# Attention kernel: inputs laid out with channels on rows, key sums by matmul, GpSimd's order written out

## The chip, the cores and the metric

The kernel runs on one core of a Trainium2 chip as a single launch. The metric is the device time of one execution in microseconds (us), lower is better; runs are compared by their medians. The engines are named as in the profile: PE is TensorE (PEld its weight loads), DVE is VectorE, ACT is ScalarE, POOL is GpSimd, SP is the queue of SyncE, which issues nearly all DMAs.

## The reference

Three stages follow each other: linear attention with an exponential feature map, a dense MLP, and a mixture of eight experts of which each token uses one. The change touches the attention, and in the others only the order of tokens.

```python
# q, k, v: (4, 8, 576, 64), w_phi: (64, 128)
def phi(x):
    proj = einsum('bhsd,df->bhsf', x, w_phi)
    proj = proj - max(abs(proj), axis=-1, keepdims=True)
    return concatenate([exp(proj), exp(-proj)], axis=-1)
q_p, k_p = phi(q), phi(k)
kv  = einsum('bhsf,bhsd->bhfd', k_p, v)
z   = sum(k_p, axis=2)
num = einsum('bhsf,bhfd->bhsd', q_p, kv)
den = einsum('bhsf,bhf->bhs', q_p, z)[..., None] + 1e-06
x = (num / den)                       # -> (2304 tokens, 512)
# MLP: h = x @ w_in; x = (h * clip(h+3,0,6)/6) @ w_out
# experts: argmax gate picks 1 of 8; relu(x @ w1[e]) @ w2[e], scaled by the gates
```

## The kernel before

**Units.** The attention works on 16 units: one batch entry and one pair of heads each. A unit holds 2 x 576 rows of q and as many of k, as nine blocks of 128 rows and two heads (blocks 0 to 3 keys, 4 the last 64 positions of both, 5 to 8 queries). Products that need more than one pass of precision are made of two halves: a value is rounded to `hi` (type fp32r), and `lo` is what is left.

**One unit's steps**, by the two-letter names that the order string `seq` uses:

- T0 to T2 (`tr_in`): TensorE transposes three blocks each (L273), so that channels lie on the partitions; ACT copies the result out of PSUM as `hi` (L276), DVE subtracts for `lo` (L278).
- P0 to P4 (`proj`): three matmuls per block (hi by hi, hi by lo, lo by hi; L294 to L296); DVE takes the largest absolute value (L300) and subtracts it (L302), giving `dd`.
- E0 to E2 (`kexp`): ACT makes both exponentials of the keys, `kp` (L309 to L313).
- S (`z_sum`): POOL adds the four key blocks of a head into `ks` (L332 to L334).
- KV (`kv_mm`): ten matmuls of `kp` with `v` into `pkv` (L324). Z (`z_mm`): four matmuls with ones, on `ks` and on the last block, into the other half of `pkv` (L342), in four groups of 32 columns of the array. C copies `pkv` out (L349); KT transposes it (L356) and makes `kvz` (ACT, L360) and `zs` (DVE, L362).
- Q0 to Q2 (`q_tr`): the queries are transposed (L378, L383); ACT makes their exponentials `qp` (L381, L386).
- N0, N1 (`num`): numerators (L431), copied into `xT` (L439). D (`den`): denominators (L396), `dn` on DVE (L406), of which four rows go by DMA into the 128-row tile `rt` (L408).
- R (`den2`, for the unit before): reciprocal (L413), DMA to DRAM, two DMAs that spread it over the partitions as `rr` (L418), and a multiply of `xT` by it on POOL (L421).
- w (`split_w`): one of the 16 pieces of the MLP's first weight half, read as 64-bit floats, becomes two fp32r halves: four DVE operations (L157, L160, L162, L164) beside a square on ACT (L158); L164 zeroes what is too small. Then a copy (L172, for two pieces on ACT, L170) and a subtraction (L173) on POOL.

**Order.** Within `tc.manual_schedule` the instructions of the engines named run in the order in which the code emits them; here these are TensorE, DVE and ACT. POOL's order and that of the DMAs on SP are the framework's. Iteration `it` runs KV, Z, Q, N, D of unit `it`, P and E of unit `it+1`, T of unit `it+2`, and loads unit `it+3` with seven DMAs. Two iterations (-2, -1) fill the pipeline; the last two have strings of their own. PSUM banks are given out by tags: two for transposes, three for P, one for KV, two for N and D.

**Afterwards** the MLP starts with six chunks of 384 tokens: L540 is its first matmul. It needs the first weight half, and while it runs its first chunk the second half is converted by the same `split_w`. Then tokens are listed by expert, and the experts run. `pieces` gives the rows of DRAM for a block of columns, as the columns of a unit are not in the order of tokens.

## Time and profile before

| | before |
|---|---|
| median of three runs | 943.39 us (943.04, 943.39, 945.1) |
| profiled execution | 944.11 us, of it span 942.0 us |
| mean granted clock of TensorE | 0.992 |
| busy share: PE / PEld / DVE / ACT / POOL | 96% / 79% / 65% / 55% / 37% |
| moved by DMA | 85.72 MB, mean 91 GB/s |

Times in the rows are us from the span's start unless marked ns. The share of a whole span is a mean over stages with different limits: in the attention DVE is nearly as busy as TensorE, in the experts it is not, so a stage has to be read by itself.

### The profile page before, as it was taken

What the parts mean: (1) busy time and instruction counts of PE and PEld (TensorE: products, weight loads), DVE (VectorE), ACT (ScalarE), POOL (GpSimd) and SP (SyncE); (2) the same over time, 40 slices, a digit from 0 to 9 for tenths busy, and PEclk for the clock granted to TensorE, in tenths of its full rate; (3) what the DMA queues carried; (4) which work ended last, traced back from release to release, by engine and by line L of the source; (5) the groups of instructions that cost most, each with busy time, mean ns of one, the idle gap of its engine ahead of it and who ended that gap; (6) DMA issues with size and microseconds to landing.
All of it is one profiled execution on the core that took longest, in us unless ns stands there. A gap on an engine that the chain in (4) does not pass through costs nothing. (4 is left out here: it accounts for less than half of the span.)

```text
span 942.0 us, 14999 instructions
## 1 busy us (share of the span) xinstructions
PE 903.5 (96%) x5250; PEld 740.3 (79%) x5250; DVE 615.8 (65%) x1033; ACT 518.9 (55%) x919; POOL 350.4 (37%) x246
## 2 busy tenths in 40 slices
...
GB/s 162 183 140 134 138 124 138 97 49 132 117 133 5 1 68 1 1 34 1 1 35 0 1 34 1 28 185 21 58 54 215 175 252 42 215 107 204 194 142 19
DMA packets 54349, 85.72 MB, mean 91 GB/s; under 512 B 18037, under 2 KB 30969, under 8 KB 54269
## 3 DMA queue, kind: packets, MB, share of 16 engines
...
## 5 line engine op out<-in xcount | busy, mean ns | idle before, releaser
L543 DVE SCALAR_TENSOR_TENSOR t<-t,ph 128x384 f32<-128x384 f32 x96 | 53.0, 552 | 159.8 <-ACT t L542 159.8
L542 ACT ACTIVATE t<-ph,b 128x384 f32<-128x384 f32 x96 | 55.7, 580 | 164.9 <-PE ph L540 164.9
L680 POOL DMA_INDIRECT lst<-ids,pi x18 | 17.8, 986 | 237.2 <-DVE pi L677 230.8
L548 ACT ACTIVATE gh<-t 128x384 fp32r<-128x384 f32 x96 | 50.4, 525 | 84.4 <-DVE t L543 81.6
L847 DVE TENSOR_TENSOR wl<-raw,wh 128x1024 fp32r<-128x1024 f32 x63 | 76.1, 1245 | 9.5 <-ACT wh L846 9.3
L552 DVE TENSOR_TENSOR gl<-t,gh 128x384 fp32r<-128x384 f32 x86 | 48.0, 558 | 46.2 <-ACT gh L548 45.6
L846 ACT ACTIVATE wh<-raw 128x1024 fp32r<-128x1024 f32 x72 | 73.0, 1070 | 4.8 <-DMA raw<-in_moe_w 4.8
L540 PE MATMUL ph<-xh,wi0A 128*128 128x384 f32 x192 | 67.6, 352 | 1.6 <-DVE t L543 1.6
L540 PE MATMUL ph<-xl,wi0A 128*128 128x384 f32 x192 | 64.7, 337 | 1.2 <-DVE xl L531 1.2
L540 PE MATMUL ph<-xh,wi1B 128*128 128x384 f32 x192 | 64.6, 336 | 0.9 <-POOL wi1B L173 0.9
L540 PE MATMUL ph<-xh,wi0B 128*128 128x384 f32 x192 | 64.8, 338 | 0.1
L540 PE MATMUL ph<-xh,wi1A 128*128 128x384 f32 x192 | 64.6, 337 | 0.0
L540 PE MATMUL ph<-xl,wi0B 128*128 128x384 f32 x192 | 64.4, 335 | 0.0
L567 PE MATMUL po<-wo1B,gh 128*128 128x512 f32 x144 | 57.3, 398 | 1.3 <-POOL wo1B L173 1.3
L300 DVE TENSOR_REDUCE mx<-pj 128x4 f32<-128x512 f32 (+1 forms) x80 | 50.4, 630 | 11.9 <-PE pj L296 11.8
L567 PE MATMUL po<-wo0B,gh 128*128 128x512 f32 x144 | 57.0, 396 | 0.6 <-ACT wo0B L170 0.6
L567 PE MATMUL po<-wo1A,gh 128*128 128x512 f32 x144 | 56.6, 393 | 0.0
L567 PE MATMUL po<-wo0A,gh 128*128 128x512 f32 x144 | 56.6, 393 | 0.0
L332 POOL TENSOR_TENSOR ks<-kp 128x512 f32<-128x512 f32 x16 | 20.9, 1307 | 89.0 <-ACT kp L310 89.0
L847 DVE TENSOR_TENSOR wi1A<-raw,wi0A 128x1024 fp32r<-128x1024 f32 x42 | 50.0, 1221 | 5.6 <-ACT wi0A L846 5.5
L847 DVE TENSOR_TENSOR wo1A<-raw,wo0A 128x1024 fp32r<-128x1024 f32 x41 | 50.6, 1265 | 3.6 <-ACT wo0A L846 3.5
L302 DVE TENSOR_TENSOR dd<-pj,mx 128x512 f32<-128x512 f32 (+1 forms) x80 | 51.0, 638 | 2.8
...
## 6 DMA issues: line engine op xcount, KB each, us to landing
...
```

Source lines behind the costliest of these rows:

```text
L300: nc.vector.tensor_reduce(m, pv, axis=AX.X, op=ALU.max, apply_absolute_value=True)
L302: nc.vector.tensor_sub(dv, pv, m.unsqueeze(2).broadcast_to([P, 2 * n, P]))
L332: nc.gpsimd.tensor_add(ks, k4[:, :, 0, 0], k4[:, :, 0, 1])
L540: nc.tensor.matmul(ph[:, 0:T], l[:, d, fs], r[:, d, :], start=(d == 0 and i == 0), stop=(d == 3 and i == 2))
L542: nc.scalar.activation(g, ph[:, 0:T], AF.Relu, bias=b3)
L543: nc.vector.scalar_tensor_tensor(g, g, 6.0, ph[:, 0:T], op0=ALU.min, op1=ALU.mult)
L548: nc.scalar.activation(gh, g, AF.Copy)
L552: (nc.gpsimd if 4 < n < 15 else nc.vector).tensor_sub(gl, g, gh.bitcast(F32))
L567: nc.tensor.matmul(pos[c][j], l[:, js], wo[r], start=(f == 0 and r == 0 and l is gh), stop=(f == 15 and l is gl))
L680: sc = nc.gpsimd.indirect_dma_start(lst, bass.IndirectOffsetOnAxis(ap=pi[:, j : j + 1], axis=0), ids[:, m : m + 1], None, bounds_check=NL - 1,
L846: nc.scalar.activation(hi, raw[i], AF.Copy)
L847: (nc.gpsimd if i == 7 or (s, i) == (0, 6) else nc.vector).tensor_sub(lo, raw[i], hi.bitcast(F32))
```

## The change

- The host lays the inputs out anew (`lay_out`): q and k of a unit as one array `qk` of 128 rows (two heads by 64 channels) by nine blocks of 128 positions, v as ten blocks with the zeros of the last two already in place, `w_phi` as the block-diagonal matrix. A unit is two DMAs (unit 0's `qk` three). Columns are now in the order of tokens, so `pieces` goes.
- T goes. In its place H (`cut`): POOL copies three blocks of `qk` to `hi` and subtracts for `lo`. For unit 0 (`h`) ACT and DVE do it. One filling iteration remains.
- S goes. Z has ten matmuls instead of four: every key block is summed with ones on TensorE.
- `split_w` for the first weight half: ACT takes the absolute value, POOL the maximum with a bound (`TINY`), and three DVE operations remain; the copy is POOL's for all pieces. For the second half nothing changes.
- All PSUM tiles of the attention share one tag of eight banks.
- POOL joins the engines with a written order. The order strings are new: KV first, the five P in one block, H behind them, R in two parts (the reciprocal and its DMAs early, the multiply late). In `kv_tr`, DVE's `zs` comes before ACT's `kvz`.

```diff
--- before.py
+++ after.py
...
@@ -154,23 +138,35 @@
     yield
     f = pool.tile([P, n], U32, tag=tags[0], bufs=tags[2], name=f"f_{nm}")
     m = pool.tile([P, n], F32, tag=tags[1], bufs=tags[2], name=f"m_{nm}")
-    nc.vector.tensor_scalar(f, hw, 3, 0x3FFFFFFF, op0=ALU.logical_shift_left, op1=ALU.bitwise_and)
-    nc.scalar.activation(m, hw.bitcast(F32), AF.Square)
-    yield
-    nc.vector.scalar_tensor_tensor(f, lw, 29, f, op0=ALU.logical_shift_right, op1=ALU.bitwise_or)
-    yield
-    nc.vector.scalar_tensor_tensor(f, hw, 0xC0000000, f, op0=ALU.bitwise_and, op1=ALU.bitwise_or)
-    yield
-    nc.vector.scalar_tensor_tensor(
-        m, m, TINY * TINY, f.bitcast(F32), op0=ALU.is_ge, op1=ALU.mult
-    )
+    if act:
+        nc.vector.tensor_scalar(f, hw, 3, 0x3FFFFFFF, op0=ALU.logical_shift_left, op1=ALU.bitwise_and)
+        nc.scalar.activation(m, hw.bitcast(F32), AF.Square)
+        yield
+        nc.vector.scalar_tensor_tensor(f, lw, 29, f, op0=ALU.logical_shift_right, op1=ALU.bitwise_or)
+        yield
+        nc.vector.scalar_tensor_tensor(f, hw, 0xC0000000, f, op0=ALU.bitwise_and, op1=ALU.bitwise_or)
+        yield
+        nc.vector.scalar_tensor_tensor(
+            m, m, TINYB * TINYB, f.bitcast(F32), op0=ALU.is_ge, op1=ALU.mult
+        )
+        f = m
+    else:
+        nc.scalar.activation(m, hw.bitcast(F32), AF.Abs)
+        nc.gpsimd.tensor_scalar(m, m, TINY, None, op0=ALU.max)
+        yield
+        nc.vector.tensor_scalar(f, m.bitcast(U32), 3, 0x3FFFFFFF, op0=ALU.logical_shift_left, op1=ALU.bitwise_and)
+        yield
+        nc.vector.scalar_tensor_tensor(f, lw, 29, f, op0=ALU.logical_shift_right, op1=ALU.bitwise_or)
+        yield
+        nc.vector.scalar_tensor_tensor(f, hw, 0xC0000000, f, op0=ALU.bitwise_and, op1=ALU.bitwise_or)
+        f = f.bitcast(F32)
     if act == 1:
         yield
     if act:
-        nc.scalar.activation(hi, m, AF.Copy)
+        nc.scalar.activation(hi, f, AF.Copy)
     else:
-        nc.gpsimd.tensor_copy(hi, m)
-    nc.gpsimd.tensor_sub(lo, m, hi.bitcast(F32))
+        nc.gpsimd.tensor_copy(hi, f)
+    nc.gpsimd.tensor_sub(lo, f, hi.bitcast(F32))
 
 
 def weight_tiles(pool, nm):
...
@@ -210,72 +206,43 @@
         pl = E(name="apl", bufs=2, side="left")
         p3 = E(name="ap3", bufs=1, side="left")
         ps = E(name="aps", bufs=1, space=PS)
-        pn = E(name="apn", bufs=1, space=PS)
-        q, k, v, w = a["q"], a["k"], a["v"], a["w_phi"]
         wbd = cst.tile([P, 256], F32, name="wbd")
-        nc.vector.memset(wbd, 0.0)
         whi = cst.tile([P, 256], F32R, name="whi")
         wlo = cst.tile([P, 256], F32R, name="wlo")
         ones = cst.tile([P, 3, 32], F32, name="ones")
         nc.gpsimd.memset(ones, 1.0)
         nc.gpsimd.memset(ones[64:128, 1, :], 0.0)
         nc.gpsimd.memset(ones[0:64, 2, :], 0.0)
-        vms = []
-        for i in range(4):
-            vm = cst.tile([P, 2, 64], F32, name=f"vm{i}")
-            nc.gpsimd.memset(vm, 0.0)
-            vms.append(vm)
         rscr = tc.dram_tile([NU, P, 9], F32, name="rscr")
 
         def load(u):
-            b, hp = divmod(u, 4)
-            ts = {}
-            for nm, src in (("k", k), ("q", q), ("v", v)):
-                t = p2.tile([P, 2, 4, 64], F32, tag="l" + nm, bufs=4 if nm == "v" else 2, name=f"{nm}{u}")
-                nc.sync.dma_start(
-                    t.rearrange("p h r d -> p h (r d)"),
-                    src[b, 2 * hp : 2 * hp + 2, 0:512, :].rearrange("h (p r) d -> p h (r d)", r=4),
-                )
-                ts[nm] = t
-                if nm == "k" and u == 0:
-                    nc.sync.dma_start(wbd[0:64, 0:128], w)
-                    nc.sync.dma_start(wbd[64:128, 128:256], w)
-                if nm == "q":
-                    qkm = load_rest(u, b, hp)
-            for h in range(2):
-                nc.sync.dma_start(vms[u % 4][64 * h : 64 * h + 64, h, :], v[b, 2 * hp + h, 512:576, :])
-            return [ts["q"], ts["k"], ts["v"], qkm, vms[u % 4]]
-
-        def load_rest(u, b, hp):
-            qkm = p2.tile([P, 2, 64], F32, tag="qkm", name=f"qkm{u}")
-            for i, src in enumerate((q, k)):
-                nc.sync.dma_start(qkm[:, i, :], src[b, 2 * hp : 2 * hp + 2, 512:576, :])
-            return qkm
+            x = p2.tile([P, 9, P], F32, tag="qk", bufs=2, name=f"qk{u}")
+            if u == 0:
+                nc.sync.dma_start(wbd, a["w_phi"])
+                for g in range(3):
+                    nc.sync.dma_start(x[:, 3 * g : 3 * g + 3], a["qk"][u][:, 384 * g : 384 * g + 384])
+            else:
+                nc.sync.dma_start(x.rearrange("p n t -> p (n t)"), a["qk"][u])
+            t = p2.tile([P, 10, 64], F32, tag="lv", bufs=4, name=f"v{u}")
+            nc.sync.dma_start(t.rearrange("p n d -> p (n d)"), a["v"][u])
+            return [x, t]
 
         hl, st, bk, rts = {}, {}, {}, {}
 
-        def tr_in(u, g):
-            Q, K, V, QKM, vm = lds[u]
+        def cut(u, g):
+            x = lds[u][0]
             if g == 0:
                 hl[u] = (
                     p1.tile([P, 9, P], F32R, tag="hi", name=f"hi{u}"),
                     p1.tile([P, 9, P], F32R, tag="lo", name=f"lo{u}"),
                 )
             hi, lo = hl[u]
-            pt = ps.tile([P, 512], F32, tag="tr", bufs=2, name=f"pt{u}_{g}")
-            for j in range(3):
-                n = 3 * g + j
-                if n == 4:
-                    src = QKM
-                else:
-                    t, n = (K, n) if n < 4 else (Q, n - 5)
-                    src = t[:, n // 2, 2 * (n % 2) : 2 * (n % 2) + 2, :]
-                nc.tensor.transpose(pt[:, j * P : (j + 1) * P], src.rearrange("p a d -> p (a d)"), ident)
-            yield
             sl = slice(3 * g, 3 * g + 3)
-            nc.scalar.activation(hi[:, sl, :], pt[:, 0:384], AF.Copy)
-            yield
-            nc.vector.tensor_sub(lo[:, sl, :], pt[:, 0:384], hi[:, sl, :].bitcast(F32))
+            if u:
+                nc.gpsimd.tensor_copy(hi[:, sl], x[:, sl])
+            else:
+                nc.scalar.activation(hi[:, sl], x[:, sl], AF.Copy)
+            (nc.gpsimd if u else nc.vector).tensor_sub(lo[:, sl], x[:, sl], hi[:, sl].bitcast(F32))
 
         def proj(u, g):
             hi, lo = hl[u]
@@ -288,7 +255,7 @@
             dd, kp, mx = st[u]
             grp = [2 * g, 2 * g + 1] if g < 2 else ([4] if g == 2 else [2 * g - 1, 2 * g])
             n = len(grp)
-            pj = ps.tile([P, 512], F32, tag="pj", bufs=3, name=f"pj{u}_{g}")
+            pj = ps.tile([P, 512], F32, tag="b", bufs=8, name=f"pj{u}_{g}")
             for j, bl in enumerate(grp):
                 o = pj[:, 256 * j : 256 * j + 256]
                 nc.tensor.matmul(o, hi[:, bl, :], whi, start=True, stop=False)
@@ -313,35 +280,34 @@
                 nc.scalar.activation(kp[:, 4, 0, 1, :], dd[:, 4, 1, :], AF.Exp, scale=-1.0)
 
         def kv_mm(u):
-            V, vm = lds[u][2], lds[u][4]
+            V = lds[u][1]
             kp = st[u][1]
-            pkv = ps.tile([P, 512], F32, tag="kv", bufs=1, name=f"pkv{u}")
+            pkv = ps.tile([P, 512], F32, tag="b", bufs=8, name=f"pkv{u}")
             bk.setdefault(u, {})["pkv"] = pkv
             for r in range(5):
                 for h in range(2):
-                    l = V[:, h, r, :] if r < 4 else vm[:, h, :]
+                    l = V[:, 4 * h + r] if r < 4 else V[:, 8 + h]
                     m = kp[:, 2 * h + r // 2, r % 2] if r < 4 else kp[:, 4, 0]
                     nc.tensor.matmul(
                         pkv[64 * h : 64 * h + 64, 0:256], l, m.rearrange("p s f -> p (s f)"), start=(r == 0), stop=(r == 4)
                     )
 
-        def z_sum(u):
-            kp = st[u][1]
-            ks = p2.tile([P, 2, 2 * P], F32, tag="kvs", bufs=1, name=f"ks{u}")
-            k4 = kp[:, 0:4].rearrange("p (h a) e s f -> p h a e (s f)", h=2)
-            nc.gpsimd.tensor_add(ks, k4[:, :, 0, 0], k4[:, :, 0, 1])
-            nc.gpsimd.tensor_add(ks, ks, k4[:, :, 1, 0])
-            nc.gpsimd.tensor_add(ks, ks, k4[:, :, 1, 1])
-            bk.setdefault(u, {})["ks"] = ks
-
         def z_mm(u):
-            pkv, kp, ks = bk[u]["pkv"], st[u][1], bk[u]["ks"]
-            for h in range(2):
-                l2 = kp[:, 4, 0].rearrange("p s f -> p (s f)")
-                for g, l, m in ((2 * h, ones[:, 0, :], ks[:, h, :]), (2 * h + 1, ones[:, 1 + h, :], l2)):
-                    nc.tensor.matmul(
-                        pkv[32 * g : 32 * g + 32, 256:512], l, m, start=True, stop=True, tile_position=(0, 32 * g)
-                    )
+            pkv, kp = bk[u]["pkv"], st[u][1]
+            for r in ((4, 3), (0, 2), (1,)):
+                for h in range(2):
+                    for e, n in enumerate(r):
+                        g = 2 * h + e
+                        l = ones[:, 1 + h if n == 4 else 0, :]
+                        m = kp[:, 4, 0] if n == 4 else kp[:, 2 * h + n // 2, n % 2]
+                        nc.tensor.matmul(
+                            pkv[32 * g : 32 * g + 32, 256:512],
+                            l,
+                            m.rearrange("p s f -> p (s f)"),
+                            start=n > 2,
+                            stop=n in (1, 2),
+                            tile_position=(0, 32 * g),
+                        )
 
         def kv_cp(u):
             pkv = bk[u]["pkv"]
...
@@ -416,6 +382,7 @@
             rv = rscr[u].rearrange("(h t) k -> h (t k)", h=2)
             for h in range(2):
                 nc.sync.dma_start(rr[64 * h : 64 * h + 64, :], rv[h : h + 1].broadcast_to([64, S]))
+            yield
             b, hp = divmod(u, 4)
             xsl = xT[:, hp, S * b : S * b + S]
             nc.gpsimd.tensor_mul(xsl, xsl, rr)
...
@@ -439,18 +406,21 @@
             nc.scalar.activation(xsl[:, cs], po[:, 0:288], AF.Copy)
 
         lds, cv = {}, {}
-        seq = "Q0 P0 P0 Q0 E0 w w P1 P1 R Q1 Q1 KV w Z Q2 C P2 P2 Q2 E1 P3 KT KT E2 P3 KT P4 T0 T0 T0 w N1 P4 N0 N0 T1 T1 T2 T1 S N1 T2 D T2 D".split()
-        pre2 = "T0 T0 T0".split()
-        pre1 = "P0 t1 t1 P0 t1 t2 t2 t2 P1 E0 P1 P2 P3 E1 P2 E2 P3 T0 P4 T0 T0 T1 T1 T1 P4 T2 T2 T2".split()
-        seq14 = "Q0 P0 P0 Q0 E0 w w P1 P1 R Q1 Q1 KV w Z C Q2 P2 P2 P3 P3 KT Q2 KT E2 E1 KT P4 w N1 P4 N0 S N1 N0".split()
-        seq15 = "Q0 d Q0 Q1 d Q1 KV w w Z C w w Q2 KT KT Q2 KT N0 R N1 N0 D N1 D".split()
-        with tc.manual_schedule(engines={nc.tensor.engine, nc.vector.engine, nc.scalar.engine}):
-            for it in range(-2, NU):
-                if it == 0:
-                    z_sum(0)
-                if it == -2:
-                    lds[0] = load(0)
-                    nc.vector.tensor_copy(whi, wbd)
+        seq = (
+            "KV Z C Q0 Q0 Q1 Q1 Q2 Q2 KT KT KT R P0 P0 P1 P1 E0 P2 P2 E1 E2 P3 P3 P4 P4 H0 H1 H2 w "
+            "N0 N0 N1 N1 D D w R w w"
+        ).split()
+        pre1 = "h0 P0 P0 h1 P1 P1 E0 P2 P2 E1 E2 h2 P3 P3 P4 P4 H0 H1 H2".split()
+        seq14 = [op for op in seq if op != "D"]
+        seq15 = "w KV Z C Q0 Q0 d Q1 Q1 d Q2 Q2 KT KT KT R w N0 N0 N1 N1 D D w R w".split()
+        with tc.manual_schedule(
+            engines={nc.tensor.engine, nc.vector.engine, nc.scalar.engine, nc.gpsimd.engine}
+        ):
+            for it in range(-1, NU):
+                if it == -1:
+                    for u in range(2):
+                        lds[u] = load(u)
+                    nc.scalar.activation(whi, wbd, AF.Copy)
                     nc.vector.tensor_sub(wlo, wbd, whi.bitcast(F32))
                 if it in (1, 4):
                     late(it)
@@ -461,25 +431,22 @@
                     cv[it + 1] = split_piece(tc, p3, a, wA, 0, it + 1, ("wf", "wm", 1))
                     step(cv[it + 1])
                 gens = {}
-                for op in {-2: pre2, -1: pre1, NU - 2: seq14, NU - 1: seq15}.get(it, seq):
+                for op in {-1: pre1, NU - 2: seq14, NU - 1: seq15}.get(it, seq):
                     kd, i = op[0], int(op[1]) if op[-1].isdigit() else 0
                     if op in gens:
                         step(gens[op])
                     elif kd == "P" and nx:
                         gens[op] = proj(it + 1, i)
                         step(gens[op])
-                    elif kd == "T" and nn:
-                        gens[op] = tr_in(it + 2, i)
-                        step(gens[op])
-                    elif kd == "t":
-                        gens[op] = tr_in(it + 1, i)
-                        step(gens[op])
+                    elif kd == "H" and nn:
+                        cut(it + 2, i)
+                    elif kd == "h":
+                        cut(it + 1, i)
                     elif kd == "E" and nx:
                         kexp(it + 1, i)
                     elif kd == "R" and it >= 1:
-                        den2(it - 1)
-                    elif kd == "S" and nx and has:
-                        z_sum(it + 1)
+                        gens[op] = den2(it - 1)
+                        step(gens[op])
                     elif kd == "Z" and has:
                         z_mm(it)
                     elif kd == "C" and has:
...
@@ -1222,6 +1188,27 @@
     return raw[i].rearrange("p (c f) -> p c f", c=2), src
 
 
+def lay_out(arrays):
+    import numpy as np
+
+    q, k, v, w = (arrays.pop("in_" + n) for n in ("q", "k", "v", "w_phi"))
+    pair = lambda x: x.reshape(NU, 2, S, D)
+    q, k, v = pair(q), pair(k), pair(v)
+    qk = np.empty((NU, 2, D, 9, P), np.float32)
+    for n, x in ((0, k), (5, q)):
+        x = x[:, :, 0:512].reshape(NU, 4, 2, P, D)
+        qk[:, :, :, n : n + 4] = x.transpose(0, 2, 4, 1, 3)
+    for i, x in enumerate((q, k)):
+        qk[:, i, :, 4] = x[:, :, 512:].transpose(0, 3, 1, 2).reshape(NU, D, P)
+    vv = np.zeros((NU, P, 10, D), np.float32)
+    vv[:, :, 0:8] = v[:, :, 0:512].reshape(NU, 2, 4, P, D).transpose(0, 3, 1, 2, 4).reshape(NU, P, 8, D)
+    wb = np.zeros((P, 2, P), np.float32)
+    for h in range(2):
+        vv[:, 64 * h : 64 * h + 64, 8 + h] = v[:, h, 512:]
+        wb[64 * h : 64 * h + 64, h] = w
+    return {"in_qk": qk.reshape(NU, P, 9 * P), "in_v": vv.reshape(NU, P, 10 * D), "in_w_phi": wb.reshape(P, 2 * P)}
+
+
 _INS = [
     "q", "k", "v", "w_phi", "moe_w_in", "moe_w_out", "moe2_w_gate", "moe2_w_output_gate", "moe2_w1", "moe2_w2",
 ]
...
```

## Rows read from the trace of the kernel before

**Rows 1.** Windows: length; busy PE, PEld, DVE, ACT, POOL; granted clock; DMA share; GB/s.

```profile
46.42:197.32 150.90, 146.60 (x1309) 102.61 (x1308) 136.47 (x246) 100.98 (x240) 88.87 (x72) 1.00 0.45 126
109.29:121.86 12.57, 12.21 (x111) 8.54 (x110) 11.32 (x21) 8.41 (x20) 7.42 (x7) 1.00 0.47 138
218.42:942.00 723.58, 701.87 (x3510) 599.80 (x3506) 429.25 (x702) 379.25 (x592) 233.70 (x139) 0.99 0.25 79
```

**Rows 2.** Timeline of PE in that unit: start, duration, instruction, idle before.

```profile
109.29 1.95 PE L324 MATMUL pkv<-kp,v 128*64 128x256 f32 x16
...
111.60 0.40 PE L342 MATMUL pkv<-ks,ones 128*32 128x256 f32 x1
...
112.17 0.33 PE L383 MATMUL pq<-ident,dd 128*128 128x128 f32 x1
112.25 0.36 PE L294 MATMUL pj<-whi,hi 128*128 128x256 f32 x1
112.45 0.28 PE L295 MATMUL pj<-wlo,hi 128*128 128x256 f32 x1
112.57 0.28 PE L296 MATMUL pj<-whi,lo 128*128 128x256 f32 x1
...
114.56 0.49 PE L273 MATMUL pt<-ident,k 128*128 128x128 f32 x3
114.98 2.16 PE L431 MATMUL po<-qp,kvz 128*64 128x288 f32 x16
117.07 0.33 PE L273 MATMUL pt<-ident,k 128*128 128x128 f32 x1
...
117.88 1.18 PE L396 MATMUL pd<-qp,zs 128*32 128x288 f32 x16
119.41 0.66 PE L378 MATMUL pq<-ident,dd 128*128 128x128 f32 x4 [0.36 <-DVE lo L278]
```

**Rows 3.** Groups by line of that unit, DVE and POOL: count, busy us, mean ns.

```profile
L278 DVE TENSOR_TENSOR lo<-pt,hi 128x384 fp32r<-128x384 f32 x3 | 1.6, 549 | 0.2 <-ACT hi L276 0.2
L164 DVE SCALAR_TENSOR_TENSOR m_i<-m_i,f_i 128x512 f32<-128x512 f32 x1 | 1.4, 1423 | 0.0
...
L157 DVE TENSOR_SCALAR f_i<-raw_i 128x512 uint32<-128x512 uint32 x1 | 0.4, 415 | 0.0
...
L421 POOL TENSOR_TENSOR xT<-xT,rr 128x576 f32<-128x576 f32 x2 | 2.8, 1419 | 0.0
...
L332 POOL TENSOR_TENSOR ks<-kp 128x512 f32<-128x512 f32 x1 | 1.3, 1311 | 4.9 <-ACT kp L310 4.9
...
L172 POOL CAST wo0A<-m_o 128x512 fp32r<-128x512 f32 x6 | 3.7, 611 | 0.0
```

**Rows 4.** Timeline of POOL and DVE late in the attention.

```profile
206.70 1.28 POOL L334 TENSOR_TENSOR ks<-ks,kp 128x512 f32<-128x512 f32 x1
...
206.98 1.29 DVE L157 TENSOR_SCALAR f_o<-raw_o 128x512 uint32<-128x512 uint32 x1
```

**Rows 5.** Groups by line of POOL in the first MoE chunk.

```profile
L552 POOL TENSOR_TENSOR gl<-t,gh 128x384 fp32r<-128x384 f32 x10 | 14.6, 1460 | 0.0
```

**Rows 6.** Timeline of PE and DVE, from the start to the first MoE matmul.

```profile
5.49 0.41 PE L295 MATMUL pj<-wlo,hi 128*128 128x256 f32 x1
...
6.96 0.69 DVE L300 TENSOR_REDUCE mx<-pj 128x4 f32<-128x512 f32 x1 [1.31 <-PE pj L296]
...
17.49 1.95 PE L324 MATMUL pkv<-kp,v 128*64 128x256 f32 x16
...
37.03 0.22 DVE L413 RECIPROCAL rt<-rt 128x9 f32<-128x9 f32 x1 [3.92 <-DMA rt<-dn]
...
207.06 1.95 PE L324 MATMUL pkv<-kp,v 128*64 128x256 f32 x16
...
213.57 3.81 PE L431 MATMUL po<-qp,kvz 128*64 128x288 f32 x16 [2.19 <-ACT kvz L360]
...
218.42 0.45 PE L540 MATMUL ph<-xh,wi0A 128*128 128x384 f32 x1
```

More of the change, by code (lines that the diff above doesn't have):

```diff
@@ L34 @@
 BIG = 1.0e6
-TINY = 3.4332275390625e-05
+TINY = 2.0**-15
+TINYB = 3.4332275390625e-05
 C_ID = 0
@@ L55, in make_consts @@
     c = np.zeros((P, C_N), np.float32)
-    col = np.arange(S)
-    tok = np.where(col < 512, 4 * (col % P) + col // P, col)
-    ids = (np.arange(B)[:, None] * S + tok[None, :]).reshape(NBLK, P)
-    c[:, C_ID : C_ID + NBLK] = ids.T
+    c[:, C_ID : C_ID + NBLK] = np.arange(NT).reshape(NBLK, P).T
     c[:, C_BASE : C_BASE + NE] = np.arange(NE) * NT
@@ L74, in make_consts @@
     return c
-def pieces(m):
-    res, c = [], P * m
-    while c < P * m + P:
-        b, k = divmod(c, S)
-        if k < 512:
-            n, t0, st = P - k % P, S * b + 4 * (k % P) + k // P, 4
-        else:
-            n, t0, st = S - k, S * b + k, 1
-        n = min(n, P * m + P - c)
-        res.append((c - P * m, c - P * m + n, t0, st))
-        c += n
-    return res
 def body(tc, a, dbg=None):
@@ L190, in split_piece @@
     src = a["moe_w_out"][1024 * half + P * f : 1024 * half + P * f + P, :]
-    return split_w(tc, pool, src, wo[0][:, f, :], wo[1][:, f, :], f"o{half}_{i}", tags, 1 if half else 2 * (i > 13))
+    return split_w(tc, pool, src, wo[0][:, f, :], wo[1][:, f, :], f"o{half}_{i}", tags, half)
 def step(g):
@@ L264, in tr_in @@
             hi, lo = hl[u]
-            pt = ps.tile([P, 512], F32, tag="tr", bufs=2, name=f"pt{u}_{g}")
-            for j in range(3):
-                n = 3 * g + j
-                if n == 4:
-                    src = QKM
-                else:
-                    t, n = (K, n) if n < 4 else (Q, n - 5)
-                    src = t[:, n // 2, 2 * (n % 2) : 2 * (n % 2) + 2, :]
-                nc.tensor.transpose(pt[:, j * P : (j + 1) * P], src.rearrange("p a d -> p (a d)"), ident)
-            yield
-            sl = slice(3 * g, 3 * g + 3)
-            nc.scalar.activation(hi[:, sl, :], pt[:, 0:384], AF.Copy)
-            yield
-            nc.vector.tensor_sub(lo[:, sl, :], pt[:, 0:384], hi[:, sl, :].bitcast(F32))
+            sl = slice(3 * g, 3 * g + 3)
+            if u:
[3 more added lines that the diff above has]
+            (nc.gpsimd if u else nc.vector).tensor_sub(lo[:, sl], x[:, sl], hi[:, sl].bitcast(F32))
         def proj(u, g):
@@ L353, in kv_tr @@
             kvs = bk[u]["kvs"]
-            pk2 = ps.tile([P, 512], F32, tag="tr", bufs=2, name=f"pk2{u}")
+            pk2 = ps.tile([P, 512], F32, tag="b", bufs=8, name=f"pk2{u}")
             for j in range(4):
@@ L359, in kv_tr @@
             zs = p3.tile([P, 2, 2, 32], F32, tag="zs", bufs=2, name=f"zs{u}")
-            nc.scalar.activation(kvz.rearrange("p a b -> p (a b)"), pk2[:, 0:256], AF.Copy)
-            yield
             nc.vector.tensor_reduce(
@@ L368, in kv_tr @@
             bk[u]["kvz"], bk[u]["zs"] = kvz, zs
+            yield
+            nc.scalar.activation(kvz.rearrange("p a b -> p (a b)"), pk2[:, 0:256], AF.Copy)
         def q_tr(u, h):
@@ L374, in q_tr @@
             qp = bk[u]["qp"]
-            pq = ps.tile([P, 512], F32, tag="tr", bufs=2, name=f"pq{u}_{h}")
+            pq = ps.tile([P, 512], F32, tag="b", bufs=8, name=f"pq{u}_{h}")
             if h < 2:
@@ L391, in den @@
             zs, qp = bk[u]["zs"], bk[u]["qp"]
-            pd = pn.tile([P, 512], F32, tag="nm", bufs=2, name=f"pd{u}")
+            pd = ps.tile([P, 512], F32, tag="b", bufs=8, name=f"pd{u}")
             for s in range(2):
@@ L418, in den2 @@
                 nc.sync.dma_start(rr[64 * h : 64 * h + 64, :], rv[h : h + 1].broadcast_to([64, S]))
+            yield
             b, hp = divmod(u, 4)
@@ L426, in num @@
             xsl = xT[:, hp, S * b : S * b + S]
-            po = pn.tile([P, 512], F32, tag="nm", bufs=2, name=f"po{u}_{c}")
+            po = ps.tile([P, 512], F32, tag="b", bufs=8, name=f"po{u}_{c}")
             cs = slice(288 * c, 288 * c + 288)
@@ L713, in r_gate @@
             yield
-            for p0, p1, t0, st in pieces(NB * c + j):
-                nc.sync.dma_start(x2d[t0 : t0 + (p1 - p0 - 1) * st + 1 : st, :], rws[c][j][p0:p1, :])
+            m = NB * c + j
+            nc.sync.dma_start(x2d[P * m : P * m + P, :], rws[c][j])
     def first_expert(n):
```

4 lines of the change are left out of this document (2 added, 2 removed).

## Prediction

> **What bounds the kernel now.** I read the windows view first, to split the span. The attention stage ends and the MoE begins at the first matmul of L540, 218.42 us into the span [rows 6]. From there to the end TensorE is busy 701.87 of 723.58 us [rows 1], and none of that code is edited. The sums over experts come out alike, too: with the drawn inputs both token orders give the same first expert (number 6) and 22 blocks of 128 tokens. So the change can act only before 218.42 us and on what is handed over there.
>
> Attention works through 16 units (one batch entry, two heads). The reader should take one unit from the steady middle, between two first pkv matmuls, 109.29 to 121.86: 12.57 us, with TensorE busy 12.21, DVE 11.32, ACT 8.41, POOL 7.42 [rows 1]. The window of twelve units, 46.42 to 197.32, gives 150.90 us, twelve times the same, at a granted clock of 1.00 (the 2.4 GHz level) and a DMA share of 0.45. Two engines are nearly full, so I looked at who waits: TensorE's only idle stretch in the unit is 0.36 us, where it waits for DVE's `lo` (L278) [rows 2]. TensorE sets the period, DVE is just behind it. What matters is therefore what the change does to TensorE's work per unit, and whether another engine passes it.
>
> **The change, part by part.**
>
> *TensorE, per unit.* The timeline of its matmuls gives each phase from its first start to the next phase's first start [rows 2]. The nine input transposes (L273) take 114.98 - 114.56 = 0.42 and 117.88 - 117.07 = 0.81, together 1.23 us: they go. The z sums (L342) take 112.17 - 111.60 = 0.57 us today for four matmuls of 256 columns which start almost together in four column groups. Afterwards there are ten, in rounds of four, four and two. A round cannot be cheaper than a pair of the neighbouring L324 phase, whose five pairs, also 256 columns, take 2.31 us, 0.46 each; so three rounds cost 1.4 to 1.7 (three times 0.57), and I take 1.5: plus 0.93. If instead the groups did not overlap at all, each of the ten would take about its 0.40 us; the eight records of L342 inside 0.57 us speak against that. The projections come in one block instead of three. The first L294 matmul of a block starts 0.20 us before the next one, the others 0.12 apart (112.25, 112.45, 112.57): two such steps fewer, minus 0.16. The 0.36 us wait on L278 goes with the transposes. Sum: 12.57 - 1.23 + 0.93 - 0.16 - 0.36 = 11.75. What is late next is any of the waits below; for these I add 0.1 and take 11.85 (bounds 11.6, all phases at their cheapest, and 12.3, below).
>
> *DVE, per unit.* It loses three `lo` subtractions of 0.55 and the masking multiply L164 of 1.42 [rows 3]: 11.32 - 1.65 - 1.42 = 8.25. It is no longer near the bound unless it is made to wait. One wait is new in place: the reciprocal of R now stands ahead of all five projection reductions, and it waits for the `rt` transfer that follows `dn` of the unit before. It once waited 3.92 us for that, up to 37.03 [rows 6]. In the new order KV takes 2.3, Z 1.5, Q and KT with thirteen transposes 1.7 (at the 1.23 for nine above), so the projections start 5.5 us into a unit. `dn` of D, the last phase, ends about 0.6 us into the next unit, and the reciprocal stands behind KT, at about 5.7; the reductions may slip another 1.4 us before the next KV misses its exponentials, so some 6 us of transfer are covered. Loads shrink from seven DMAs on the SP queue to two, so the `rt` DMA has fewer ahead of it.
>
> The other wait is on POOL. L157, the first weight operation, took 1.29 us at 206.98, where POOL was in the middle of an addition (L334) [rows 4], against 0.42 in the steady unit [rows 3]. If each of the three remaining weight operations grows by these 0.87, DVE stands at 8.25 + 2.6 = 10.9, below 11.85. If each waits out a whole POOL instruction of 1.42, it stands at 12.5 and is the bound. I take the lower, since in the new order POOL has only the multiply of R to run beside these three, and then itself waits for the last of them. The Trainium skill, SBUF — State Buffer, "SBUF: two separate sides", says that DVE and GpSimd share one port pair as an exclusive lock, whoever comes first holding it for its whole instruction. The row agrees with that: L157 ended 0.3 us after the addition it met.
>
> *POOL, per unit.* It loses the three additions of L332 to L334, about 1.3 us each [rows 3, 4], 4 in all. It gains three copies and three subtractions of 128x384, and one 128x512 maximum. A copy of 128x512 (L172) takes 0.61 [rows 3], so 0.46 for 384; a two-input operation on 512 takes 1.31, so 0.98, while the same shape in the MoE stage beside a full DVE (L552) took 1.46 [rows 5]. The cuts cost 4.3 to 5.8. The maximum has no row: between 0.6 (one input, like L172) and 1.5 (like L552); I take 0.8. With the multiply L421 (1.42), the copy L172 (0.61) and its subtraction (1.31, two inputs of 512) POOL has 8.4, at most 10.6 us. The place in the order matters more than the sum: H0 can start when P1's matmuls have read the old halves, 1.5 us of matmuls after the projections begin, so about 7 us into the unit, and H2 has to be ready for the next unit's P3, some 12 us later, for 4.3 us of work. The maximum, behind them, is due when DVE reaches the weight operations at about 12.5; it is done at about 12. The multiply (R's second step) sits behind that and hides the round trip of the reciprocals through DRAM. All of it is covered at these prices.
>
> The Trainium skill, GPSIMD Engine Reference, "Engine selection", advises against elementwise work on this engine (about twice as slow with two inputs). Here 0.98 stands against DVE's 0.55, which agrees. It speaks against the change only if POOL becomes the bound; that is a rival below.
>
> *ACT* loses three copies of its 8.41 us. *DMA*: as many bytes in longer rows, with a share of 0.45; costed at nothing.
>
> *The start.* Today KV of unit 0 starts at 17.49, after transposes of three units [rows 6]. The new first load is a weight block and one third of the input, no more bytes than today's first two, so I keep 6.96 for the first reduction. Then DVE goes P0 1.3 (the 0.69 of L300 there and a subtraction as wide), lo 0.55, P1 1.3, P2 0.8: 10.9; two exponentials of block 4 and two of P1 on ACT to 12.2, the third cut 12.2 to 13.2, nine matmuls 1.3: KV of unit 0 at 14.5. Gain 3.0 (bounds 0 and 5).
>
> *Units 0 to 2.* Today 46.42 - 17.49 = 28.93, with that wait of 3.92 on DVE inside. Afterwards 2 x 11.85, plus 1.5 for matmuls at the pace of the first ones (L295 0.41 us at 5.49, against 0.28 at 112.45 [rows 2, 6], though the granted clock reads 1.00 in both places), with bounds 0 and 4 (a wait like today's): 25.2. Gain 3.7.
>
> *Units 2 to 14.* 150.90 against 12 x 11.85 = 142.2. Gain 8.7.
>
> *Unit 14.* Today 207.06 - 197.32 = 9.74, as it has no transposes and no denominators. Afterwards it lacks only the denominators (119.05 - 117.88 = 1.17): 10.7. Loss 0.9.
>
> *Unit 15 to the MoE.* Today 11.36, with a 2.19 us wait for `kvz` and numerator matmuls that then took 3.81 us instead of 2.16 [rows 2, 6]. Afterwards: two denominators, and about 1.4 us of wait for `kvz` behind four exponentials: 11.3. Gain 0.1.
>
> Sum: 3.0 + 3.7 + 8.7 - 0.9 + 0.1 = 14.6. The profiled execution took 944.11, of which 942.0 is span; it lies 0.7 above the median of 943.39. So 929.5 for that execution and 929 for the median.
>
> **The rivals.**
>
> *The unit does not get to TensorE's bound.* The reciprocal's transfer, a wait on POOL or a copy holds the projections, and the unit takes 12.3. Over fourteen units this costs 0.45 x 14 = 6.3: 935. For it: the one stall that the trace shows is of this kind. Against it: DVE and ACT have 3 us to spare in each unit.
>
> *POOL becomes the bound, and the kernel slower.* It decides from 12.57 us of POOL per unit, beyond the 10.6 of the dearest rows. If the 384 copies cost what a two-input operation costs beside a full DVE (1.46 for 0.46, three times), POOL has 10.6 + 3.0 = 13.6: 14 x (13.6 - 12.57) = 14 more than now, less the 3 of the start: 955. Against it: L172 is measured in this very stage.
>
> *The gain is given back at the handover.* In the first MoE chunk TensorE waits for the second half of the weights, which DVE converts. If their loads or tiles are not free earlier, the MoE starts earlier only to wait: within 2 us of 943. Against it: those pieces follow attention's own end in the same queues.
>
> *More than that.* The unit comes to 11.6, the start and units 0 to 2 go without slow matmuls and stall: 0.25 x 12 + 1.5 + 2 = 6 more: 923.
>
> **How the numbers follow.** The forecast has 0.55, the unit short of the bound 0.2, the larger gain 0.15, the handover 0.05, POOL 0.05. The median is 929; the likeliest case alone reaches from 925 to 933. The range 922 to 938 takes in the rival at 935 and the larger gain, and leaves out the last two. A change of 0.2%, 1.9 us, is about what a measurement here can tell from none: faster 0.91, same 0.04, slower 0.05.
>
> **What would show it.** Right: no L273 rows, a unit of about 11.8 us with TensorE almost without pause, L342's successor at about 1.5 us per unit, DVE near 9 busy, POOL's cuts near 1.4 each, the first L540 matmul at about 204. Wrong: TensorE waiting for `hi` or `lo` (POOL), for `kp` (DVE held by the reciprocal or by POOL), a z phase above 2 us, or a first MoE chunk longer by what attention gained.

## The result, and the profile after

| | changed kernel |
|---|---|
| median of four runs | 930.77 us (930.58 to 932.8) |
| kernel before, same chip, four runs | 943.92 us (943.04 to 945.1) |
| ratio | 0.9865, 95% interval 0.9847 to 0.9883 |
| profiled execution | 930.91 us, of it span 929.1 |

The changed kernel is 13 us faster; 929 was forecast. Its windows, in the columns of [rows 1], are one unit, twelve units, the second 10 us of the first MoE chunk, and the MoE from its first matmul on:

```profile
109.46:121.19 11.73, 11.73 (x116) 8.15 (x113) 9.71 (x17) 7.16 (x18) 9.17 (x11) 1.00 0.51 149
39.10:179.94 140.84, 140.84 (x1348) 97.77 (x1344) 116.42 (x197) 85.55 (x204) 110.16 (x121) 1.00 0.46 142
213.22:223.22 10.00, 9.47 (x40) 8.73 (x41) 9.16 (x16) 4.16 (x8) 3.55 (x2) 0.83 0.36 117
203.22:929.10 725.88, 703.18 (x3506) 601.28 (x3506) 431.46 (x702) 378.97 (x591) 233.88 (x141) 0.99 0.25 79
```

The length and TensorE's busy time are equal in the unit and over twelve units: the trace shows TensorE no idle time in 140.84 us, where it had 4.3 in the 150.90 before [rows 1]. The timeline of TensorE, at the places of [rows 6], shows the first KV, the z phase of unit 14 with the phase behind it, and the end of the attention:

```profile
14.79 3.23 PE L291 MATMUL pkv<-kp,v 128*64 128x256 f32 x20
...
182.25 1.50 PE L303 MATMUL pkv<-kp,ones 128*32 128x256 f32 x20
183.68 1.09 PE L344 MATMUL pq<-ident,dd 128*128 128x128 f32 x8
...
190.46 2.33 PE L291 MATMUL pkv<-kp,v 128*64 128x256 f32 x20
...
198.77 2.16 PE L398 MATMUL po<-qp,kvz 128*64 128x288 f32 x16 [1.73 <-ACT kvz L334]
...
203.22 0.41 PE L507 MATMUL ph<-xh,wi0A 128*128 128x384 f32 x1 [1.18 <-issue]
...
213.75 0.44 PE L507 MATMUL ph<-xh,wi0A 128*128 128x384 f32 x1 [1.96 <-DVE t L510]
```

The z phase takes 183.68 - 182.25 = 1.43 us. The MoE starts at 203.22, that is 15.2 us earlier than at 218.42; 725.88 - 723.58 = 2.3 us of it are lost again behind that point. DVE's and POOL's timelines in the unit, where the change put most of its new work:

```profile
112.45 1.64 DVE L157 TENSOR_SCALAR f_i<-m_i 128x512 uint32<-128x512 uint32 x1 [1.71 <-POOL m_i L155]
114.12 0.69 DVE L159 SCALAR_TENSOR_TENSOR f_i<-raw_i,f_i 128x512 uint32<-128x512 uint32 x1
114.84 0.69 DVE L161 SCALAR_TENSOR_TENSOR f_i<-raw_i,f_i 128x512 uint32<-128x512 uint32 x1
115.45 0.42 DVE L326 TENSOR_REDUCE zs<-pk 128x128 f32<-128x256 f32 x1
...
110.93 1.48 POOL L155 TENSOR_SCALAR m_i<-m_i 128x512 f32<-128x512 f32 x1
112.39 1.41 POOL L388 TENSOR_TENSOR xT<-xT,rr 128x576 f32<-128x576 f32 x1
```

L157 waits 1.71 us for POOL's maximum and then takes 1.64 beside POOL's multiply. Groups by line of POOL in the same unit give the cuts' price:

```profile
L245 POOL TENSOR_TENSOR lo<-qk,hi 128x384 fp32r<-128x384 f32 x3 | 3.0, 1012 | 0.2
L242 POOL CAST hi<-qk 128x384 fp32r<-128x384 f32 x4 | 2.0, 502 | 0.4 <-PE pj L262 0.4
```

### The profile page after: what moved, and what is told of

Read it like the earlier page. It is cut to its first block, busy times and chain, and to the rows that moved or that the text cites. A ratio compares the mean times of both kernels' runs of the same rounds, so it can differ in the third digit from the quotient of the medians.

```text
span 929.1 us, 14953 instructions
## 1 busy us (share of the span) xinstructions
PE 895.8 (96%) x5298; PEld 735.1 (79%) x5298; DVE 589.0 (63%) x970; ACT 499.1 (54%) x873; POOL 373.3 (40%) x302
## 5 line engine op out<-in xcount | busy, mean ns | idle before, releaser
L510 DVE SCALAR_TENSOR_TENSOR t<-t,ph 128x384 f32<-128x384 f32 x96 | 53.0, 552 | 159.7 <-ACT t L509 153.8
L507 PE MATMUL ph<-xh,wi0A 128*128 128x384 f32 x192 | 67.7, 353 | 3.5 <-DVE t L510 2.3
L507 PE MATMUL ph<-xl,wi0A 128*128 128x384 f32 x192 | 65.3, 340 | 1.2 <-DVE xl L498 1.2
L507 PE MATMUL ph<-xh,wi1B 128*128 128x384 f32 x192 | 64.6, 336 | 0.9 <-POOL wi1B L169 0.9
L507 PE MATMUL ph<-xh,wi1A 128*128 128x384 f32 x192 | 65.1, 339 | 0.0
L507 PE MATMUL ph<-xh,wi0B 128*128 128x384 f32 x192 | 64.8, 338 | 0.0
L507 PE MATMUL ph<-xl,wi0B 128*128 128x384 f32 x192 | 64.4, 335 | 0.0
L261 PE MATMUL pj<-whi,hi 128*128 128x256 f32 x144 | 43.4, 301 | 6.8 <-ACT hi L244 6.8
```

The costliest lines, as they stand in the source:

```text
L261: nc.tensor.matmul(o, hi[:, bl, :], whi, start=True, stop=False)
L507: nc.tensor.matmul(ph[:, 0:T], l[:, d, fs], r[:, d, :], start=(d == 0 and i == 0), stop=(d == 3 and i == 2))
L510: nc.vector.scalar_tensor_tensor(g, g, 6.0, ph[:, 0:T], op0=ALU.min, op1=ALU.mult)
```

## The experiments

The theory: TensorE's own instructions set the period, before and after, and what left DVE and POOL only has to stay covered. The rival: DVE's relief (cuts and mask leave it) is the gain. Ratios are to the kernel before on the same chip; "windows" are in the columns of [rows 1].

**Two halves of the change alone, on the kernel before.** The first lets only the z sums go to TensorE; `z_sum` and S are gone:

```diff
-                for g, l, m in ((2 * h, ones[:, 0, :], ks[:, h, :]), (2 * h + 1, ones[:, 1 + h, :], l2)):
...
+            for r in ((4, 3), (0, 2), (1,)):
+                for h in range(2):
+                    for e, n in enumerate(r):
```

> The kernel before with one part of the change alone: the z sums as ten matmuls on TensorE, POOL's three additions gone, transposes kept. If TensorE's matmul work sets a unit of 12.57 us, its z phase of 0.57 grows to about 1.45 and the unit to 13.4, so the kernel is slower by 15 x 0.85 = 13: about 957. If DVE sets the unit, TensorE has slack for it and the time stays within 3 of 944.

Measured: 948.94 us, ratio 1.0046 (1.0033 to 1.0059). A window of one unit:

```profile
110.09:123.11 13.02, 13.02 (x123) 9.08 (x122) 10.78 (x21) 8.49 (x20) 3.26 (x3) 1.00 0.46 135
```

The z phase grew by 0.86 us, the unit by 0.45, to TensorE's full 13.02: the other 0.4 was the idle time on `lo` of [rows 2], now filled. In the profiled executions the span grew by some 5 us: from the first KV to that of unit 15 the units took 194.7 us for 189.6, so 5.1 more; the start came 0.4 earlier, KV of unit 15 to the MoE took 8.82 for 11.36, and the MoE took 2.8 more. POOL's 4 us less and DVE's 0.5 less bought nothing in the unit. The sign is the theory's; its 957 is missed by far, as it left out the idle time and the end, and 949 lies nearer to the rival's time. What speaks for the theory here is the unit, with no idle time on TensorE left in it.

The second takes only the new `split_w` (`if act: ... else: ...`, as in the diff of the change) into the kernel before.

> The kernel before with the new weight split alone: DVE loses the multiply of 1.42 us per unit, POOL gains a maximum of about 1.5. If TensorE sets the unit, only its wait of 0.36 us on lo can go: 15 x 0.36 = 5, so 939 to 944. If DVE sets it, the unit falls by up to 1.2 us: about 926 to 930.

Measured: 967.72 us, ratio 1.0237 (1.0204 to 1.027), which neither theory foresaw. A window of one unit, the two instructions from POOL's and DVE's timelines, and TensorE's waits in the unit:

```profile
118.31:132.58 14.27, 12.55 (x110) 8.58 (x110) 10.10 (x20) 8.58 (x20) 8.90 (x8) 1.00 0.41 125
...
120.53 1.49 POOL L172 TENSOR_SCALAR m_i<-m_i 128x512 f32<-128x512 f32 x1 [2.08 <-ACT m_i L171]
122.05 0.43 DVE L174 TENSOR_SCALAR f_i<-m_i 128x512 uint32<-128x512 uint32 x1 [3.37 <-POOL m_i L172]
...
123.85 0.39 PE L307 MATMUL pj<-whi,hi 128*128 128x256 f32 x1 [0.83 <-DVE dd L315]
130.12 0.66 PE L391 MATMUL pq<-ident,dd 128*128 128x128 f32 x4 [0.74 <-DVE lo L291]
```

DVE's work falls from 11.32 to 10.10 us and the unit grows by 1.70. The first weight operation now stands at the end of a chain from ACT over POOL to DVE; everything behind it in DVE's order waits 3.37 us, and TensorE waits for what comes from there (`dd`, `lo`). Less work on the second busiest engine is a loss where it adds a wait in the middle of its queue.

**The cuts back on ACT and DVE**, in the changed kernel:

```diff
-            if u:
-                nc.gpsimd.tensor_copy(hi[:, sl], x[:, sl])
...
-            (nc.gpsimd if u else nc.vector).tensor_sub(lo[:, sl], x[:, sl], hi[:, sl].bitcast(F32))
+            nc.scalar.activation(hi[:, sl], x[:, sl], AF.Copy)
+            nc.vector.tensor_sub(lo[:, sl], x[:, sl], hi[:, sl].bitcast(F32))
```

> The changed kernel with the input halves cut by ACT (copy) and DVE (subtraction) for every unit, not by POOL. If TensorE's 11.73 us of matmuls set the unit, DVE's 8.2 to 9.7 plus 1.7 to 2.5 still fit and the time stays within 3 of 931. If the move of the cuts off DVE brought the gain, DVE comes near 12 us and the unit grows by 0.5 to 1: 938 to 946.

Measured: 931.36 us, ratio 0.9851 (0.9821 to 0.9881), and a unit of

```profile
109.26:120.99 11.73, 11.73 (x117) 8.15 (x113) 11.49 (x20) 8.36 (x21) 5.08 (x4) 1.00 0.47 150
```

The same 11.73 with DVE 1.8 us busier and POOL 4.1 less. The rival falls: DVE's 11.49 is even more than its 11.32 in the kernel before, and the whole gain is there. With TensorE at the bound it is free where the cuts run, here with DVE at up to 11.49 of 11.73.

**The z sums back on POOL**, in the changed kernel, with the cuts on POOL too: `z_sum` and the four matmuls of before, and an S in the order:

```diff
-            ... E1 E2 P3 P3 P4 P4 H0 H1 H2 w "
+            ... E1 E2 P3 P3 P4 P4 S H0 H1 H2 w "
```

> The changed kernel with the z sums back on POOL (three additions, four matmuls), the cuts staying there. TensorE's unit falls to about 10.9, POOL's work rises from 9.2 to 9.2 + 4.2 = 13.4 us. If POOL becomes the bound as the rival of the prediction says, the unit is 13.4 or more and the time 931 + 15 x 1.7 = 956 or more, slower than the kernel before. If POOL's work is hidden at any size, the time falls to about 919.

Measured: 1016.14 us, ratio 1.0757 (1.0721 to 1.0793). A window of one unit, then a line of DVE's and one of TensorE's timeline:

```profile
113.33:130.67 17.34, 12.72 (x104) 8.29 (x100) 9.45 (x17) 6.98 (x17) 12.71 (x13) 0.90 0.31 95
...
122.14 1.62 DVE L157 TENSOR_SCALAR f_o<-m_o 128x512 uint32<-128x512 uint32 x1 [7.58 <-POOL m_o L155]
...
126.01 3.62 PE L399 MATMUL po<-qp,kvz 128*64 128x288 f32 x16 [4.21 <-ACT kvz L335]
```

The unit is 17.34 us, though POOL works only 12.71 of it. The waits close a ring: the additions wait for the exponentials, the maximum stands behind additions and cuts, DVE's L157 waits 7.58 us for it, `zs` and the projections stand behind L157 on DVE, and the next exponentials wait for the projections. Here the written order on ACT, POOL and DVE makes a period as long as the ring, longer than any engine's work. TensorE's granted clock, 0.90 as the mean of this window, is 0.50 (the 1.2 GHz level) from 126 to 129 us, behind the 4.21 us of idle time, and L399 takes 3.62 us for 2.16; DVE shows no wait for TensorE there, so the slower matmuls do not lengthen the ring. So the z sums on TensorE, a cost by themselves, are what lets POOL take the cuts in this order.

**The end of the attention.** Unit 15's denominators are put earlier, in the second kernel the last weight pieces too (the string of unit 15 alone):

```diff
-R w N0 N0 N1 N1 D D w R w          (changed kernel)
+D R w N0 D N0 N1 N1 w R w          (first)
+D R w w w N0 D N0 N1 N1 R          (second)
```

> The changed kernel with one move in the last unit's order: the denominators before the numerators. If the first MoE matmul waited 1.18 us for the copy of the last denominators (its bank), and TensorE's 1.73 us wait for kvz can be filled by them, the first MoE matmul comes about 2 us earlier, at 201, and the time is 929. If that wait was only code being fetched, the time stays at 931.

> As the run before, and the last weight piece's remaining steps moved ahead of the numerators, the last multiply behind them. If POOL's late copy, subtraction and multiply are what stretches DVE's operations in the first MoE chunk and lets TensorE stand 1.96 us, the chunk gets its 2.3 us back: 927. If DVE's conversions alone set that chunk, nothing further changes: 929.

Measured: 932.06 us, ratio 0.9864 (0.9844 to 0.9884), and 931.21, ratio 0.9857 (0.9836 to 0.9878): no difference from the changed kernel. In the first the wait ahead of L507 shrinks (0.51 for 1.18), but 929 is missed; the second misses both of its times. TensorE's timeline of the first, then of the second, at the start of the MoE and at the last wait of this kind:

```profile
202.46 0.44 PE L507 MATMUL ph<-xh,wi0A 128*128 128x384 f32 x1 [0.51 <-ACT xT L406]
...
233.00 0.44 PE L507 MATMUL ph<-xh,wi0A 128*128 128x384 f32 x1 [0.33 <-DVE t L510]
```

```profile
202.32 0.41 PE L507 MATMUL ph<-xh,wi0A 128*128 128x384 f32 x1 [0.84 <-ACT xT L406]
209.15 0.44 PE L507 MATMUL ph<-xh,wi0A 128*128 128x384 f32 x1 [2.05 <-DVE t L510]
...
228.23 0.44 PE L507 MATMUL ph<-xh,wi0A 128*128 128x384 f32 x1 [0.35 <-DVE t L510]
233.01 0.45 PE L507 MATMUL ph<-xh,wi0A 128*128 128x384 f32 x1 [0.30 <-DVE t L510]
```

The MoE starts 0.8 and 0.9 us earlier and is level again at 233.0; the changed kernel has this row at 232.86. In the second kernel TensorE waits for DVE's `t` at every tile from 209.15 on, 4.74 to 4.78 us apart: the first chunk goes at the pace of DVE, which converts the weights beside its work on `t` (in the changed kernel it is busy 9.2 of 10 us there). DVE's first conversion (L142) starts at 201.60 in the changed kernel, but at 203.53 and 204.44 in these two, behind `xl` (L498), which waits for the later numerators. An earlier start of the MoE is worth nothing there, as DVE's conversions come no earlier.

**Less work on TensorE again.** POOL adds one pair of key blocks, so that z needs two rounds instead of three; the maximum is moved early:

```diff
+            nc.gpsimd.tensor_add(ks, k4[:, :, 0, 0], k4[:, :, 0, 1])
...
-            for r in ((4, 3), (0, 2), (1,)):
+            for r in ((4, 3), (0, 2)):
...
-            "KV Z C Q0 ... P3 P3 P4 P4 H0 H1 H2 w "
+            "KV Z C w Q0 ... P3 P3 P4 P4 H0 H1 H2 S "
```

> The changed kernel with one addition of two key blocks back on POOL, so that the z sums take two rounds of four matmuls, and the weight maximum early in the unit. TensorE's unit falls from 11.73 to 11.25, POOL's work rises from 9.2 to 10.5, still below. If TensorE sets the unit, 15 x 0.48 = 7 less: 924. If POOL's queue at 10.5 us already holds up the cuts or the maximum, the unit stays at 11.7 or grows: 931 to 940.

Measured: 935.99 us, ratio 0.9903 (0.9883 to 0.9922): the second of the two forecasts. A window of 12 us:

```profile
109.00:121.00 12.00, 11.94 (x116) 8.03 (x114) 11.55 (x18) 7.47 (x19) 11.06 (x12) 1.00 0.49 148
```

From KV of unit 2 at 39.56 to that of unit 14 at 183.00 a unit takes 11.95. POOL (11.06) and DVE (11.55 in a stretch of 12.00) are nearly full, and in eleven units TensorE waits for `ks`, as at 126.55:

```profile
126.55 0.40 PE L313 MATMUL pkv<-ks,ones 128*32 128x256 f32 x1 [0.45 <-POOL ks L299]
```

So what the missing round saves is waited away. Two things were changed at once here, the pair sum and the place of the maximum; what each does alone was not tried. Then the copies to `hi` were put on ACT to relieve POOL:

```diff
-                nc.gpsimd.tensor_copy(hi[:, sl], x[:, sl])
+            nc.scalar.activation(hi[:, sl], x[:, sl], AF.Copy)
```

> The run before with the three copies of a cut on ACT (1.5 us more there, 8.7 in all), POOL down to 9.0. If POOL was no bound at 10.5, the same time as that run: 924. If POOL was, this is faster than that run by what it lost there.

Measured: 947.33 us, ratio 1.0024 (1.0014 to 1.0034), a miss. A line of POOL's and one of TensorE's timeline:

```profile
115.39 3.15 POOL L242 TENSOR_TENSOR lo<-qk,hi 128x384 fp32r<-128x384 f32 x3 [2.68 <-ACT hi L241]
...
120.29 0.40 PE L310 MATMUL pkv<-ks,ones 128*32 128x256 f32 x1 [1.24 <-POOL ks L296]
```

POOL has less to do (10.0 us per unit for 11.1, units 5 to 10) and finishes later: it waits 2.68 us for copies that stand behind the exponentials in ACT's order.

The last pair takes the cuts off POOL whole (ACT and DVE, as above) and lets POOL's multiply (M, the late step of R) run in the next unit behind the weight operations. The first has the pair sum, the second is the same without it:

```diff
-            "KV Z C Q0 ... E1 E2 P3 P3 P4 P4 H0 H1 H2 w "
-            "N0 N0 N1 N1 D D w R w w"
+            "KV Z C w M Q0 ... E1 E2 S P3 P3 P4 P4 H0 H1 H2 "
+            "N0 N0 N1 N1 D D w w w"
```

> One pair of key blocks is added on POOL and the z sums take two rounds instead of three; the cuts stand on ACT and DVE, which takes some 3 us per unit off POOL; absolute value and maximum of the weight piece stand before Q, and the late multiply of R stands behind the weight operations in the next unit, so that POOL has nothing to hold DVE up with there. If TensorE sets the unit once the other engines are out of its way, the unit is 11.73 less one round of 0.48 = 11.25, the z phase 0.95, POOL some 7.5 busy, and fourteen units give 6.7 us less: about 924. Rival: DVE, with the cuts' subtractions 11.5 busy in the kernel where only they were moved, is the second bound right above it: the unit stays at 11.6 or more and the time at 929 or above, TensorE waiting for dd or lo.

> The control for the pair sum: the same kernel with the z sums as in the change (three rounds). TensorE sets the unit: 11.73 as in the changed kernel, 931. DVE's L157 should take its 0.43 us alone instead of 1.64, since the maximum and the multiply lie elsewhere, and DVE some 10.5 busy instead of 11.5; if the lock had been what costs, the time falls below 929.

Measured: 926.16 us (925.47 to 927.24), ratio 0.9801 (0.9783 to 0.9819), with the pair sum; 931.99, ratio 0.9857 (0.984 to 0.9874), without. Windows of one unit, first with, then without, the latter with its L157:

```profile
106.36:117.66 11.30, 11.30 (x112) 7.90 (x108) 10.01 (x20) 8.17 (x21) 6.08 (x5) 1.00 0.51 156
```

```profile
109.19:120.92 11.73, 11.73 (x116) 8.14 (x113) 10.05 (x20) 8.21 (x21) 4.76 (x4) 1.00 0.51 150
...
111.46 0.42 DVE L157 TENSOR_SCALAR f_i<-m_i 128x512 uint32<-128x512 uint32 x1
```

One round of z less is worth 11.73 - 11.30 = 0.43 us a unit, and TensorE stays without idle time: the theory's 11.25 within 0.05. Between the two kernels, which differ in the pair sum alone, the medians differ by 5.8 us. The control has no more waits or stretched weight operations on DVE, and gains nothing by that. The kernel with the pair sum is the fastest of all; of the 6.8 us by which its MoE starts earlier than the changed kernel's (196.42), 1.4 are again lost in the MoE (727.28 us). Its control, starting at 202.69, has as long a MoE (727.5), so it is not the earlier start that costs them.

## Why the prediction was right, step by step

**The bound.** Right, and shown from both sides: with TensorE 0.86 longer the kernel before slows, with TensorE 0.43 shorter the changed kernel gains, and DVE busy 9.7, 10.0 or 11.5 gives the same 11.73.

**The unit.** Forecast 11.85 (sum 11.75 and 0.1 for waits), measured 11.73. By rows: 12.57 - 1.23 - 0.36 - 0.16 + 0.86 (z, for 0.93) = 11.68. No wait needed the 0.1. That the transposes alone bring their 1.23 was not tried by itself, nor was the new order without the rest of the change.

**POOL's prices.** Copy 0.50 and subtraction 1.01, forecast 0.46 and 0.98: right. The maximum was taken at 0.8 and took 1.48, at the dear bound; POOL came to 9.17 for 8.4. It did make DVE wait (1.71 us for the maximum, 1.2 more in L157 beside the multiply), and the cover held: `zs` at 115.45 and the projections' reductions behind it came in time. The Trainium skill, SBUF — State Buffer, "SBUF: two separate sides", says that one of the two engines holds their shared ports for a whole instruction; L157 ended 0.29 us after the multiply, and took 0.42 with POOL idle, which agrees.

**The reciprocal's transfer.** No stall: units 0 to 2 took 24.31 for 25.2, and the wait of 3.92 in [rows 6] has no successor there. The forecast's 1.5 for matmuls at the pace of the first ones came to 0.85 (24.31 less twice 11.73). The start came at 14.79 for 14.5, in part by errors that cancel: the first reduction came at 6.39 for 6.96, and the last matmuls ahead of KV took from 12.41 to 14.79, 2.4 us for 1.3.

**Unit 14 and the handover.** 10.52 for 10.7; KV of unit 15 to the MoE took 12.76 for 11.3: the wait for `kvz` was 1.73 for 1.4, and the 1.18 before L507, where the last denominators' evacuation had just ended, was not in the sum. The first MoE matmul came at 203.22 for about 204.

**Behind the handover.** Costed at nothing, cost 2.3 us. DVE's timeline of the changed kernel, with a later row of TensorE's, then the same of the kernel before:

```profile
206.24 0.55 DVE L510 SCALAR_TENSOR_TENSOR t<-t,ph 128x384 f32<-128x384 f32 x1 [0.72 <-ACT t L509]
206.71 1.53 DVE L142 TENSOR_SCALAR f_i<-raw_i 128x512 uint32<-128x512 uint32 x1
208.17 0.96 DVE L519 TENSOR_TENSOR gl<-t,gh 128x384 fp32r<-128x384 f32 x1
209.05 1.77 DVE L145 SCALAR_TENSOR_TENSOR f_i<-raw_i,f_i 128x512 uint32<-128x512 uint32 x1
...
211.66 1.57 DVE L149 SCALAR_TENSOR_TENSOR m_i<-m_i,f_i 128x512 f32<-128x512 f32 x1
213.15 0.54 DVE L510 SCALAR_TENSOR_TENSOR t<-t,ph 128x384 f32<-128x384 f32 x1
...
232.86 0.44 PE L507 MATMUL ph<-xh,wi0A 128*128 128x384 f32 x1 [0.33 <-DVE t L510]
```

```profile
221.49 0.55 DVE L543 SCALAR_TENSOR_TENSOR t<-t,ph 128x384 f32<-128x384 f32 x1 [0.35 <-ACT t L542]
221.96 1.23 DVE L157 TENSOR_SCALAR f_i<-raw_i 128x512 uint32<-128x512 uint32 x1
...
224.30 1.68 DVE L162 SCALAR_TENSOR_TENSOR f_i<-raw_i,f_i 128x512 uint32<-128x512 uint32 x1
...
226.70 0.55 DVE L543 SCALAR_TENSOR_TENSOR t<-t,ph 128x384 f32<-128x384 f32 x1
...
227.30 0.44 PE L540 MATMUL ph<-xh,wi0A 128*128 128x384 f32 x1 [0.26 <-DVE t L543]
...
246.43 0.44 PE L540 MATMUL ph<-xh,wi0A 128*128 128x384 f32 x1 [0.33 <-DVE t L543]
```

Some 1.6 of the 2.3 us are lost ahead of the row at 213.75: from the first MoE matmul to it 10.53 us pass, before 8.88 (218.42 to 227.30). From there four tiles take 19.11 us, before 19.13. Between the first two operations on `t` (L510, before L543) DVE needs 6.91 us for 5.21. Four of its operations run there beside POOL's last multiply, its copy and subtraction of the last weight piece and its first subtraction for the second half, and take 5.8 us, where they take 2.4 with POOL idle. Before, two did, 2.9 us for 1.1, as that piece was done ahead of the MoE. So the rival "given back at the handover" came true in a small part, but not for its reason: DVE waits for no load there, POOL's late work slows it. In the second kernel with the earlier denominators, where POOL's copy and subtraction come earlier, DVE goes from the first operation on `t` to the second in 4.72 us (208.56 to 213.28), but it reaches the first 2.3 us later, so nothing is won.

The granted clock, 0.50 from 214.5 to 217.9 us behind the wait of 1.96, costs nothing in this chunk: the four tiles keep their pace, and that second kernel, at a granted clock of 1.00 throughout, is at the same row at 233.01. The other 0.7 us are lost behind the chunk: from TensorE's first wait for POOL's `gl` (237.22, before 250.81) to the end the two kernels took 691.9 and 691.2 us, and the run with the copies on ACT 694.8 with the same code. Their cause stays open.

Sum: 2.7 + 4.6 + 10.1 - 0.8 - 1.4 = 15.2 at the handover, for 14.6, less 2.3. The mechanism was right; that the total came so near is in part luck, as units 2 to 14 gave 1.4 more than forecast, unit 15 cost 1.5 more, and the 2.3 had no term.

**The opposite rival.** That POOL becomes the bound did not happen at 9.17 us. With the z sums left on POOL the kernel was slower than this rival's 955, at 1016, but not as it says: POOL worked 12.71 of 17.34 us, and the ring of waits, not POOL's work, set the period.
